# Seven of layer two's weight units multiplied where they were converted, in the first token pair, with a new sequence

## The chip, the cores and the metric

The kernel runs on one core of a Trainium2 chip. The metric is the device time of a run in microseconds (us); the time before is the median of three runs. The engines are named as in the profile: PE is TensorE (PEld its weight loads), DVE is VectorE, ACT is ScalarE, POOL is GpSimd, and SP is SyncE, which here issues all of the DMAs. Each engine works through its own instructions in order.

## The reference, cut to what matters

```python
x = attention(q, k, v)               # 4 x 8 heads, 576 positions, window 32 or 32 x 4, fp32 softmax
x = x.transpose(0, 2, 1, 3).reshape(2304, 512)
h = x @ w_in1                        # layer one: 512 -> 1024
ln = layernorm(h * softmax(h)) * g_ln
y = ln @ w_out1                      # 1024 -> 512
h2 = y @ w_in2                       # layer two: 512 -> 2048
g = h2 / (1 + exp(-1.702 * h2))
out = g @ w_out2                     # 2048 -> 512, all of it fp32 in and out
```

The weights arrive as 64-bit floats and are turned into 32-bit words on the chip.

## The kernel before

Every fp32 product is made from three products of a reduced fp32 type: each operand is split into a high part (`hi`) and the rest (`lo`), and high x high, high x low and low x high are summed.

**Layer two** uses seven block products instead of eight (a Strassen-like scheme). Its 2304 tokens are cut into three *pairs* of 2 x 384 tokens (`p` = 0, 1, 2). The 2048 hidden features are eight *quads* (`q` = 0 to 7). For each pair and quad, `h_prod` (products on line 719, tiles `hx` and `hz`) makes seven products `m` = 0 to 6 of six matmuls each, and `o_prod` (line 796, tiles `ox` and `oz`) does the same for the output side, by `jj` = 0 to 7. The weights of one quad need two *units*, ('q', q, 0) and ('q', q, 1), and each unit has two halves (`part` 0 and 1: 384 and 512 KB). The output side has units ('o', jj, 0) and ('o', jj, 1).

**A unit's way** is: `unit_fetch` (line 629, 512 KB from the input), conversion from 64 to 32 bits (lines 429, 433 or 437, and 441), four sums of blocks (`unit_sum`, line 638), then for each half a `hi` copy (line 655) and a `lo` subtraction (line 659) into an `hl` tile, and `unit_store` (line 663), which writes the half to a DRAM tensor (`wdq`, `wdo`). The products of every pair read the weights back from there: `quad_load` (line 668, tiles `ws`), `o_load` (line 772, tiles `wo`) and `o_load2` (line 782, tiles `w`). The units of groups `PARK[1]` and `PARK[2]` are converted during attention in buffers lent by `y1`; the 23 of `PARK[3]` follow in three `raw` and nine `hl` rooms (six from the end of attention, three more when layer one's first products are done). The same nine `hl` rooms hold the loaded `ws` and `wo` tiles. A quad of pair 0 uses four of them: two units of two halves.

**The order of the work** is written out by hand. `plan.add` collects pieces of work, each with an engine, what it comes after, which rooms it takes and gives back, and a cost. The list `ORDER` numbers the works in the order in which `add` was called and sets the order on every engine; `PICKS` says which engine takes a work that could run on several. The costs (`W2_T` and others) serve the planner; on the chip the order and the semaphores decide. An SP instruction that waits for a room or for a `lo` half holds up all the DMAs behind it.

In pair 0 the quads run in the order 0, 1, 2, 3, 6, 5, 4, 7 on PE, between the last products of layer one (line 599) and the output side. The output side's units 3 come last.

Of the kernel before, what the change touches and what calls it, by code (L numbers as in the profile page):

```python
# [18 lines left out]
P = 128  # L19
# [147 lines left out]
def attention_moe_kernel(ctx, tc, qk, qk_last, v, v_last, masks, w_in, w_out, g_ln, w2_in, w2_out, out):  # L167
# [502 lines left out]
    def quad_weights(q, m, kk, a):  # L670

        part, k = ((0, 2), (1, 1), (1, 2), (1, 0), (0, 0), (0, 1), (1, 3))[m]
        return wst[q, kk, part][:, (2 * k + a) * P:(2 * k + a + 1) * P]
# [35 lines left out]
    def h_prod(p, q, m):  # L709
        if m == 0:  # L710
            hX[q] = [x_tile((p, q, 0), f"hx{p}_{q}_0")]
        elif m == 1:
            hX[q].append(x_tile((p, q, 1), f"hx{p}_{q}_1"))
        elif m in (2, 3):
            hZW[q, m] = psB.tile([P, 512], F32, tag="B", name=f"hz{p}_{q}_{m}")
        ps = hX[q][1 if m == 1 else 0] if m in (0, 1, 4) else hZW[q, 2 if m in (2, 5) else 3]
        for kk in range(2):
            for i, (a, x) in enumerate(((0, 0), (0, 1), (1, 0))):
                nc.tensor.matmul(ps[:, 0:TB2], quad_weights(q, m, kk, a), yc2[m][:, x, kk, :],  # L719
                                 start=(m < 4 and kk == 0 and i == 0), stop=(kk == 1 and i == 2), skip_group_check=True)  # L720
# [29 lines left out]
    def o_block(jj, half, b):  # L750
        return gst[jj, half, b]

    def o_sum(jj, i, eng):

        b11, b12, b21, b22 = (o_block(jj, h, b) for h in range(2) for b in range(2))
        o, x, y_, op = ((b12, b22, b12, ALU.subtract), (b11, b12, b11, ALU.add),
                        (b12, b22, b11, ALU.subtract), (b21, b21, b11, ALU.subtract))[i]
        eng.tensor_tensor(o, x, y_, op)  # L758
# [15 lines left out]
    seen = {}  # L774
# [9 lines left out]
    def o_prod(p, jj, m):  # L784
        k = seen[p, m] = seen.get((p, m), 0) + 1
        first, last = k == 1, k == NQ
# [4 lines left out]
        for d in range(2):  # L791
# [28 lines left out]
    def o_store(p, c):  # L820
        r, b = ((1, 1), (0, 0), (1, 0), (0, 1))[c]
        t = 2 * TB2 * p + TB2 * b
        nc.sync.dma_start(out[2 * P * r:2 * P * r + 2 * P, t:t + TB2].rearrange("(d p) t -> p d t", p=P),
                          ob[c].rearrange("p (d t) -> p d t", d=2))
# [48 lines left out]
    QK_T, V_T, L_T, W_T, W2_T = 1.35, 1.3, 1.45, 1.3, 1.4  # L873
# [119 lines left out]
    stored = {}  # L993
    for k in (1, 2, 3):
        w_after = [end[n] for n in range(4)] if k < 3 else [closed]
        raw, hl = (("raw", k), ("hl", k)) if k < 3 else ("raw", "hl")
        for n, u in enumerate(PARK[k]):
# [5 lines left out]
            w = add(r, "SP", W2_T, fetch, w_after, take=(raw,), lag=3.1)  # L1003
# [6 lines left out]
            for part in range(2):  # L1010
                fin = part == 1

                def split(copy, k=k, u=u, part=part):
# [10 lines left out]
                    r, "SP", W2_T * (1 if fin or u[0] == "o" else 0.77), lambda u=u, p=part: unit_store(u, p), [w], lag=2.0,  # L1024
                    give=(hl,))
# [52 lines left out]
    for p in range(3):  # L1078
# [4 lines left out]
        for n, q in enumerate(QUADS):  # L1083
            r = r0 + 10 * n
            ready, held = [], []
            for kk in range(2):
                for part in range(2):
                    def load(p=p, q=q, kk=kk, part=part):
# [3 lines left out]
                        r - 30, "SP", W2_T * (0.77, 1)[part], load, [stored[("q", q, kk), part], opened] + kept_hi, take=("hl",),  # L1092
# [4 lines left out]
            for m in range(7):  # L1097
# [5 lines left out]
                elif m == 6:  # L1103
                    after.extend(ms[4:])
                w = add(r, "PE", 1.042, lambda p=p, q=q, m=m: h_prod(p, q, m), after,
                        take=(("X", "Q"), ("X",), ("B",), ("B",), (), (), ())[m], give=("hl",) * 4 if m == 6 else ())
# [23 lines left out]
                for key in held if m == 6 else ():  # L1130
                    hl_end[key] = w
# [18 lines left out]
        for jj in range(NQ):  # L1150
            r = r0 + 10 * jj
            loads = []
            for d in range(2):
                def load(p=p, jj=jj, d=d):
                    o_load(jj, d, hl_tile(f"wo{p}_{jj}_{d}", hi_now[p, "o", jj, d], hl_end[p, "o", jj, d]))
                hi_now[p, "o", jj, d] = w = add(
                    r - 60, "SP", W2_T, load, [stored[("o", jj, d), 0], stored[("o", jj, d), 1]] + ready[-1:], take=("hl",),
# [40 lines left out]
        for m in (4, 5, 6):  # L1198
            xs_ = []
            for jj in range(NQ):  # L1200
                r = r0 + 10 * (NQ * (m - 3) + jj)
                if jj % 2 == 0:
# [5 lines left out]
                    hi_now[p, m, jj] = w = add(r - 60, "SP", 1.5, load,  # L1208
# [9 lines left out]
                else:  # L1218
                    last_g[jj, "g11"] = op = operand(jj, m, 1, 1, muls[jj][3:] + [gsum[jj, 0], gsum[jj, 2], now["b21", jj]],
                                                     give=("g11",))  # L1220
                x = add(r, "PE", 1.042, lambda p=p, m=m, jj=jj: o_prod(p, jj, m), [w, op] + wait[m] + end_[3],
                        give=("gs", room) if jj % 2 else ("gs",))
                if jj % 2:
                    x.after.append(xs_[-1])
                hl_end[p, m, jj - jj % 2] = x
                xs_.append(x)
# [5 lines left out]
            else:  # L1232
                cs = []
                for d in range(2):
                    cs.append(add(r, "DVE", 0.56, lambda p=p, c=m - 3, d=d: o_out(p, c, d), xs_ + cs,
                                  take=() if d else ("sg",), give=("B",) if m == 5 else ("B", "p1")))
                store(m - 3, cs)
# [5 lines left out]
def plan_sequence():  # L1243
# [29 lines left out]
    for b in range(1, B):  # L1273
        todo, k = items[b - 1], 0
        for u in range(UB):
# [36 lines left out]
PARK = {1: [('q', 4, 1), ('q', 0, 1), ('q', 3, 1)],  # L1312
# [9 lines left out]
ORDER = [10, 1, 97, 98, 99, 100, 8, 56, 57, 58, 59, 101, 60, 4, 77, 78, 5, 67, 79, 68, 61, 62, 69, 80, 81, 9, 266,  # L1322
# [248 lines left out]
```

## Time and profile before

| | us |
|---|---|
| median of 3 runs | 677.64 (676.11 to 681.71) |
| profiled execution | 675.26 |
| its span, first to last instruction | 673.5 |
| PE busy | 640.5 (95%) |
| DVE, ACT, POOL busy | 440.6, 352.2, 292.6 |
| DMA | 169.99 MB, 252 GB/s over the span |

The span is what the trace covers; the execution's time has a little more around it. A busy PE is not a PE at its peak, because matmuls overlap and their ends are modelled. The granted clock of PE (PEclk) is given as a share of full speed.

### The profile page before, as it was taken

What the parts mean: (1) busy time and instruction counts of PE and PEld (TensorE: products, weight loads), DVE (VectorE), ACT (ScalarE), POOL (GpSimd) and SP (SyncE); (2) the same over time, 40 slices, a digit from 0 to 9 for tenths busy, and PEclk for the clock granted to TensorE, in tenths of its full rate; (3) what the DMA queues carried; (4) which work ended last, traced back from release to release, by engine and by line L of the source; (5) the groups of instructions that cost most, each with busy time, mean ns of one, the idle gap of its engine ahead of it and who ended that gap; (6) DMA issues with size and microseconds to landing.
All of it is one profiled execution on the core that took longest, in us unless ns stands there. A gap on an engine that the chain in (4) does not pass through costs nothing.

```text
span 673.5 us, 14859 instructions
## 1 busy us (share of the span) xinstructions
PE 640.5 (95%) x5877; PEld 596.9 (89%) x5877; DVE 440.6 (65%) x777; ACT 352.2 (52%) x762; POOL 292.6 (43%) x343
## 2 busy tenths in 40 slices
PE   6699999999999999999778899999999999999997
PEld 3467898888998999999678899999999999999997
DVE  4888877866777766866576678643466763354764
ACT  3778867764576466544235556322465542334552
POOL 1345655566344557336135116400665461133464
PEclk9889999999999999999799999999999999999999
DMA  9995753735546756597999999686898777878882
GB/s 336 402 355 177 251 179 138 241 109 191 174 142 213 251 201 247 200 319 254 356 292 367 316 327 311 227 274 232 259 313 281 243 223 241 281 246 267 287 268 102
DMA packets 67013, 169.99 MB, mean 252 GB/s; under 512 B 7168, under 2 KB 28800, under 8 KB 66944
## 3 DMA queue, kind: packets, MB, share of 16 engines
q1 hardware_dynamic: 66944, 169.05, 74.1%
q8 instruction: 46, 0.75, 0.5%
q14 instruction: 23, 0.19, 0.1%
HBM read 132.85 MB, written 36.18 MB: 251 GB/s over the span
## 4 chain that ended last, share of the span: by engine, by line
PE 81%; DMA 9%; DVE 4%; POOL 3%; issue 2%; ACT 1%; SPq 0%; DVEq 0%; POOLq 0%; ACTq 0%
PE y L599 15%; PE h L522 15%; PE oz L796 13%; PE hz L719 11%; PE ox L796 9%; PE hx L719 8%; DMA ws<-wdq 4%; PE lt L577 2%; DMA wo<-wdo 2%; PE s L268 2%; PE ptp L351 1%; POOL gs L765 1%; PE xt L381 1%; DMA wdo<-hl_('o', 5, 1)_0_4980 1%; PE xt L384 1%
## 5 line engine op out<-in xcount | busy, mean ns | idle before, releaser
L762 ACT CAST gs<-g 128x384 fp32r<-128x384 f32 x168 | 85.1, 514 | 75.6 <-PE ox L796 27.0
L765 POOL TENSOR_TENSOR gs<-g,gs 128x384 fp32r<-128x384 f32 x64 | 69.6, 1096 | 106.5 <-ACT gs L762 91.1
L719 PE MATMUL hz<-yc,ws 128*128 128x384 f32 x576 | 112.0, 336 | 1.6 <-POOL yc L706 0.7
L719 PEld LDWEIGHTS hz<-yc,ws 128*128 128x128 f32 x576 | 101.4, 189 | 2.6 <-POOL yc L706 1.1
L719 PE MATMUL hx<-yc,ws 128*128 128x384 f32 x432 | 88.2, 342 | 10.3 <-DMA ws<-wdq 10.2
L765 DVE TENSOR_TENSOR gs<-g,gs 128x384 fp32r<-128x384 f32 x104 | 68.1, 669 | 43.8 <-ACT gs L762 43.0
L719 PEld LDWEIGHTS hx<-yc,ws 128*128 128x128 f32 x432 | 76.9, 192 | 13.0 <-DMA ws<-wdq 9.2
L599 PE MATMUL y<-lnh,wo_h 128*128 128x256 f32 x288 | 82.5, 287 | 0.0
L599 PE MATMUL y<-lnl,wo_h 128*128 128x256 f32 x288 | 81.4, 283 | 0.0
L599 PE MATMUL y<-lnh,wo_l 128*128 128x256 f32 x288 | 81.4, 283 | 0.0
L748 ACT ACTIVATE g<-g 128x384 f32<-128x384 f32 x72 | 36.6, 522 | 62.7 <-DVE g L738 30.6
L758 POOL TENSOR_TENSOR g<-g,g 128x384 f32<-128x384 f32 x31 | 34.4, 1113 | 70.2 <-ACT g L748 51.1
L522 PE MATMUL h<-wi_h,xh 128*128 128x512 f32 x144 | 58.9, 409 | 0.5 <-issue 0.5
L796 PE MATMUL ox<-gs,wo 128*128 128x384 f32 x288 | 56.2, 339 | 3.0 <-DMA wo<-wdo 2.8
L522 PE MATMUL h<-wi_l,xh 128*128 128x512 f32 x144 | 56.3, 391 | 0.0
L522 PE MATMUL h<-wi_h,xl 128*128 128x512 f32 x144 | 56.3, 391 | 0.0
L599 PEld LDWEIGHTS y<-lnh,wo_h 128*128 128x128 f32 x288 | 55.1, 191 | 0.5
L599 PEld LDWEIGHTS y<-lnl,wo_h 128*128 128x128 f32 x288 | 55.2, 192 | 0.3
L599 PEld LDWEIGHTS y<-lnh,wo_l 128*128 128x128 f32 x288 | 55.1, 191 | 0.0
L796 PEld LDWEIGHTS ox<-gs,wo 128*128 128x128 f32 x288 | 50.0, 188 | 5.3 <-issue 2.7
L796 PE MATMUL oz<-gs,wo 128*128 128x384 f32 x288 | 54.7, 336 | 0.0
L796 PE MATMUL oz<-gs,w 128*128 128x384 f32 x288 | 53.9, 337 | 0.0
(343 smaller groups left out, 1250.4 us busy)
## 6 DMA issues: line engine op xcount, KB each, us to landing
ws<-wdq SPq DMA_DIRECT2D x48, 512.0 KB, 6.0
wo<-wdo SPq DMA_DIRECT2D x48, 512.0 KB, 5.9
ws<-wdq SPq DMA_DIRECT2D x48, 384.0 KB, 5.4
w<-wdo SPq DMA_DIRECT2D x72, 256.0 KB, 5.8
qk<-in_qk_dram SPq DMA_DIRECT2D x14, 528.0 KB, 5.1
v<-in_v_dram SPq DMA_DIRECT2D x14, 512.0 KB, 5.7
y<-in_w_in_dram SPq DMA_DIRECT2D x9, 512.0 KB, 4.8
wdq<-y SPq DMA_DIRECT2D x9, 512.0 KB, 6.5
```

What stands on the lines that cost most here:

```text
L268: nc.tensor.matmul(ps[QB * j:QB * j + QB, h, m * KW:m * KW + KW], q_[rows, c:c + QB], k_[rows, c:c + KW], start=not masked, stop=not maske ...
L351: nc.tensor.transpose(ps[:, j * P:j * P + P], t[:, 2 * j:2 * j + 2, :].rearrange("p m k -> p (m k)"), ident)
L381: nc.tensor.matmul(o, w, pt[rows, x:x + QB].rearrange("p (r t) -> p r t", r=4), start=True, stop=True, tile_position=(64 * par, 64 * h))
L522: nc.tensor.matmul(hps[i][:, half, :], x[:, kt, :], w[:, kt, fs], start=(kt == 0 and j == 0), stop=(kt == KT - 1 and j == 2))
L577: nc.tensor.transpose(ps[:, j, :], es[i][:, f * P:f * P + P], ident)
L599: nc.tensor.matmul(yps[g, dm][:, 0:n], w[:, f, ds_], x[:, f, 0:n], start=(f == 0 and j == 0), stop=(f == NF1 - 1 and j == 2))
L719: nc.tensor.matmul(ps[:, 0:TB2], quad_weights(q, m, kk, a), yc2[m][:, x, kk, :], start=(m < 4 and kk == 0 and i == 0), stop=(kk == 1 and i ...
L748: nc.scalar.activation(g_tile(q, 0, 0) if (half, b) == (0, 0) else src, src, AF.Gelu_apprx_sigmoid)
L758: eng.tensor_tensor(o, x, y_, op)
L762: nc.scalar.copy(gsp[jj, m][:, 0], o_block(jj, half, b))
L765: eng.tensor_tensor(gsp[jj, m][:, 1], o_block(jj, half, b), f32(gsp[jj, m][:, 0]), ALU.subtract)
L796: nc.tensor.matmul(ps, w, gsp[jj, m][:, x], start=m < 4 and first and i == 0, stop=last and i == 2, skip_group_check=True)
```

## The change

The seven units ('q', 1, 1) to ('q', 7, 1) are listed in `KEPT`. In pair 0 the products read their halves from the `hl` tiles in which they were split; they are still stored, since pairs 1 and 2 load them. A kept room is given back when the quad's last product and the store are both done. `PARK` is dealt anew: the units ('q', q, 0) and ('q', 0, 1) come in the lent buffers, and `PARK[3]` holds all the `o` units and the seven kept ones. The loads of `wo` in pair 0 no longer come after the last `ws` load of the planner's list. In the last pair, the last output product (`m` = 6) is cut for `jj` from 4 on: first all of `d` = 0, then all of `d` = 1, and its result is stored in two halves. The planner's costs for DMAs are set anew and `ORDER` and `PICKS` are other lists.

```diff
-    def quad_weights(q, m, kk, a):
+    def quad_weights(p, q, m, kk, a):
         part, k = ((0, 2), (1, 1), (1, 2), (1, 0), (0, 0), (0, 1), (1, 3))[m]
+        if p == 0 and ("q", q, kk) in KEPT:
+            return hls[("q", q, kk), part][:, (2 * k + a) * P:(2 * k + a + 1) * P]
         return wst[q, kk, part][:, (2 * k + a) * P:(2 * k + a + 1) * P]
...
-    def o_store(p, c):
+    def o_store(p, c, d0=0, nd=2):
         r, b = ((1, 1), (0, 0), (1, 0), (0, 1))[c]
-        t = 2 * TB2 * p + TB2 * b
-        nc.sync.dma_start(out[2 * P * r:2 * P * r + 2 * P, t:t + TB2].rearrange("(d p) t -> p d t", p=P),
-                          ob[c].rearrange("p (d t) -> p d t", d=2))
+        t, e = 2 * TB2 * p + TB2 * b, (2 * r + d0) * P
+        nc.sync.dma_start(out[e:e + nd * P, t:t + TB2].rearrange("(d p) t -> p d t", p=P),
+                          ob[c].rearrange("p (d t) -> p d t", d=2)[:, d0:d0 + nd])
...
-    QK_T, V_T, L_T, W_T, W2_T = 1.35, 1.3, 1.45, 1.3, 1.4
+    QK_T, V_T, L_T, W_T, W2_T = 1.35, 1.3, 1.45, 1.3, 1.45
...
                 stored[u, part] = hl_end[u, part] = x = add(
-                    r, "SP", W2_T * (1 if fin or u[0] == "o" else 0.77), lambda u=u, p=part: unit_store(u, p), [w], lag=2.0,
-                    give=(hl,))
+                    r, "SP", 1.35 if fin or u[0] == "o" else 1.1, lambda u=u, p=part: unit_store(u, p), [w], lag=2.1,
+                    give=() if u in KEPT else (hl,))
+                split_of[u, part] = w
...
                 for part in range(2):
+                    u = "q", q, kk
+                    if p == 0 and u in KEPT:
+                        ready.append(split_of[u, part])
+                        held.append((u, part))
+                        continue
...
                 for key in held if m == 6 else ():
-                    hl_end[key] = w
+                    hl_end[key] = w if len(key) == 4 else add(r, None, 0, lambda: None, [w, stored[key]], give=("hl",))
...
-                    r - 60, "SP", W2_T, load, [stored[("o", jj, d), 0], stored[("o", jj, d), 1]] + ready[-1:], take=("hl",),
+                    r - 60, "SP", W2_T, load, [stored[("o", jj, d), 0], stored[("o", jj, d), 1]] + (ready[-1:] if p else []), take=("hl",),
...
+                if p == 2 and m == 6 and jj >= NQ // 2:
+                    for d in range(2):
+                        x = add(r + 100 * d, "PE", 0.521, lambda p=p, m=m, jj=jj, d=d: o_prod(p, jj, m, (d,)),
+                                [w, op] + wait[m] + end_[3] + xs_[:1] + by_d[0][-1:],
+                                give=(("gs", room) if jj % 2 else ("gs",)) if d else ())
...
+                if by_d[0]:
+                    s0 = add(r, "SP", 0.7, lambda p=p, c=m - 3: o_store(p, c, 0, 1), cs[:1], lag=3.0)
+                    add(r, "SP", 0.7, lambda p=p, c=m - 3: o_store(p, c, 1, 1), cs[1:] + [s0], give=("sg",), lag=3.0)
...
-PARK = {1: [('q', 4, 1), ('q', 0, 1), ('q', 3, 1)],
-        2: [('q', 4, 0), ('q', 3, 0), ('q', 1, 0), ('q', 2, 1), ('q', 6, 0), ('q', 5, 0)],
-        3: [('q', 0, 0), ('q', 7, 1), ('q', 7, 0), ('q', 5, 1), ('q', 2, 0), ('q', 1, 1), ('o', 0, 0), ('o', 0, 1),
...
+PARK = {1: [('q', 0, 0), ('q', 0, 1), ('q', 1, 0)],
+        2: [('q', 2, 0), ('q', 3, 0), ('q', 4, 0), ('q', 5, 0), ('q', 6, 0), ('q', 7, 0)],
+        3: [('o', 0, 0), ('o', 4, 1), ('o', 1, 0), ('o', 2, 1), ('o', 0, 1), ('q', 1, 1), ('o', 6, 0), ('o', 7, 0), ('o', 6, 1),
...
+KEPT = [('q', q, 1) for q in range(1, 8)]
```

`ORDER` and `PICKS` are replaced as a whole (2435 works before, 2440 after) and are not shown.

## Rows read from the trace of the kernel before

**Rows 1.** The page, busy tenths of PE and DMA in 40 slices.

```profile
PE   6699999999999999999778899999999999999997
DMA  9995753735546756597999999686898777878882
```

**Rows 2.** Windows: from:to length, busy us by engine, PEclk, DMA share, GB/s.

```profile
0.00:41.92 41.92, 29.68 (x832) 19.79 (x833) 28.77 (x50) 24.97 (x64) 11.24 (x16) 0.88 0.98 369
41.92:302.77 260.85, 259.44 (x3077) 233.60 (x3072) 194.91 (x350) 167.08 (x367) 140.09 (x195) 1.00 0.60 207
302.77:400.82 98.05, 84.33 (x454) 80.16 (x454) 65.59 (x123) 42.97 (x87) 31.57 (x39) 0.97 0.94 317
400.82:669.57 268.75, 267.00 (x1521) 263.39 (x1521) 150.75 (x255) 117.17 (x246) 109.66 (x96) 1.00 0.78 257
669.57:673.50 3.93, 0.00 (x1) 0.00 (x0) 0.60 (x2) 0.00 (x0) 0.00 (x0) 1.00 0.28 100
```

**Rows 3.** Longest wait of PE on loads: total us, times, longest.

```profile
PE hx L719 <- DMA ws<-wdq: 10.2, 7, 4.0
```

**Rows 4.** Timeline of PE: start, length, instruction, idle before.

```profile
302.77 1.20 PE L719 MATMUL hx<-yc,ws 128*128 128x384 f32 x6
303.81 1.20 PE L719 MATMUL hz<-yc,ws 128*128 128x384 f32 x6
331.48 4.21 PE L719 MATMUL hx<-yc,ws 128*128 128x384 f32 x12 [4.00 <-DMA ws<-wdq]
400.82 0.79 PE L796 MATMUL ox<-gs,wo 128*128 128x384 f32 x3 [0.54 <-DMA wo<-wdo]
```

**Rows 5.** Windows inside the stretch of layer two's first pair.

```profile
320.00:337.00 17.00, 12.12 (x53) 11.17 (x52) 8.49 (x17) 4.48 (x9) 1.85 (x4) 0.80 1.00 357
354.00:371.00 17.00, 15.09 (x85) 14.28 (x84) 11.16 (x21) 8.92 (x18) 9.40 (x12) 1.00 1.03 363
```

**Rows 6.** The chain that ended last: start, length, what.

```profile
316.81 0.92 DVE raw_('o', 4, 0)_4435 L638
319.52 6.89 DMA wdo<-hl_('o', 4, 0)_0_4715
326.42 5.01 DMA ws<-wdq
349.93 7.97 DMA wdo<-hl_('o', 5, 1)_0_4980
357.92 4.38 DMA ws<-wdq
```

**Rows 7.** DMA issues of the page, and all landings of L668.

```profile
ws<-wdq SPq DMA_DIRECT2D x48, 512.0 KB, 6.0
DMA to landing us min/median/max: 3.3/5.7/9.1
```

**Rows 8.** Timeline: fetch, first and last conversion of unit ('o', 3, 1).

```profile
358.81 0.37 SPq L629 DMA_DIRECT2D raw_('o', 3, 1)_5070<-in_w_out_dram  x1
365.32 0.68 ACT L437 ACTIVATE raw_('o', 3, 1)_5070<-raw_('o', 3, 1)_5070 128x512 uint32<-128x512 uint8 x1 [0.45 <-DMA raw_('o', 3, 1)_5070<-in_w_out_dram]
372.77 0.69 DVE L659 TENSOR_TENSOR hl_('o', 3, 1)_1_5208<-raw_('o', 3, 1)_5070,hl_('o', 3, 1)_1_5208 128x512 fp32r<-128x512 f32 x1
```

**Rows 9.** Groups by line, 300 to 400 us: two `lo` halves on DVE.

```profile
L659 DVE TENSOR_TENSOR hl_('o', 4, 0)_0_4715<-raw_('o', 4, 0)_4435,hl_('o', 4, 0)_0_4715 128x512 fp32r<-128x512 f32 x1 | 1.4, 1395 | 0.0
L659 DVE TENSOR_TENSOR hl_('o', 5, 0)_0_4882<-raw_('o', 5, 0)_4683,hl_('o', 5, 0)_0_4882 128x512 fp32r<-128x512 f32 x1 | 0.7, 684 | 0.0
```

**Rows 10.** Timeline: the last products and the last two drains.

```profile
656.57 13.00 PE L796 MATMUL oz<-gs,w 128*128 128x384 f32 x72
669.09 1.08 DVE L818 TENSOR_TENSOR ob<-oz,op 128x384 f32<-128x384 f32 x2 [3.41 <-PE oz L796]
```

**Rows 11.** The start: a window, and the last `lo` that gates layer one.

```profile
17.00:34.00 17.00, 11.88 (x338) 8.65 (x335) 14.05 (x25) 12.09 (x32) 5.43 (x5) 0.87 1.03 399
33.76 2.40 POOL L491 TENSOR_TENSOR wi_l<-w1r,wi_h 128x1024 fp32r<-128x1024 f32 x1 [3.53 <-DVE wi_h L478]
```

More of the change, by code (lines that the diff above doesn't have):

```diff
@@ L718, in h_prod @@
             for i, (a, x) in enumerate(((0, 0), (0, 1), (1, 0))):
-                nc.tensor.matmul(ps[:, 0:TB2], quad_weights(q, m, kk, a), yc2[m][:, x, kk, :],
+                nc.tensor.matmul(ps[:, 0:TB2], quad_weights(p, q, m, kk, a), yc2[m][:, x, kk, :],
                                  start=(m < 4 and kk == 0 and i == 0), stop=(kk == 1 and i == 2), skip_group_check=True)
@@ L753, in o_sum @@
     def o_sum(jj, i, eng):
-        b11, b12, b21, b22 = (o_block(jj, h, b) for h in range(2) for b in range(2))
+        b11, b12, b21, b22 = ((h, b) for h in range(2) for b in range(2))
         o, x, y_, op = ((b12, b22, b12, ALU.subtract), (b11, b12, b11, ALU.add),
                         (b12, b22, b11, ALU.subtract), (b21, b21, b11, ALU.subtract))[i]
-        eng.tensor_tensor(o, x, y_, op)
+        eng.tensor_tensor(o_block(jj, *o), o_block(jj, *x), o_block(jj, *y_), op)
     def o_hi(p, jj, m, half, b):
@@ L782, in o_load2, with o_prod @@
             nc.sync.dma_start(f32(t[:, k]), wd["o", jj + k].rearrange("p (d c) -> p d c", d=2)[:, :, at_:at_ + 2 * P])
-    def o_prod(p, jj, m):
-        k = seen[p, m] = seen.get((p, m), 0) + 1
-        first, last = k == 1, k == NQ
+    def o_prod(p, jj, m, ds=(0, 1)):
+        for d in ds:
+            seen[p, m, d] = seen.get((p, m, d), 0) + 1
+        first, last = seen[p, m, ds[0]] == 1, seen[p, m, ds[0]] == NQ
         if first and m < 2:
@@ L790, in o_prod @@
             oZ[m] = [psB.tile([P, 512], F32, tag="B", name=f"oz{p}_{m}_{d}") for d in range(2)]
-        for d in range(2):
+        for d in ds:
             ps = (oX[1 if m == 1 else 0][d] if m in (0, 1, 4) else oZ[2 if m in (2, 5) else 3][d])[:, 0:TB2]
@@ L990, in attention_moe_kernel @@
     ended = add(-1, None, 0, end_y, list(yc.values()))
-    stored = {}
+    stored, split_of = {}, {}
     for k in (1, 2, 3):
@@ L1002, in fetch @@
                     [P, 1024], F32, tag="raw", bufs=NRAW, name=f"raw_{u}")).bitcast(U32))
-            w = add(r, "SP", W2_T, fetch, w_after, take=(raw,), lag=3.1)
+            w = add(r, "SP", 1.6, fetch, w_after, take=(raw,), lag=3.2)
             if w2[u[0]].dtype == I64:
@@ L1091, in attention_moe_kernel @@
                     hi_now[p, q, kk, part] = w = add(
-                        r - 30, "SP", W2_T * (0.77, 1)[part], load, [stored[("q", q, kk), part], opened] + kept_hi, take=("hl",),
+                        r - 30, "SP", (1.15, 1.45)[part], load, [stored[("q", q, kk), part], opened] + kept_hi, take=("hl",),
                         lag=3.0)
@@ L1105, in attention_moe_kernel @@
                 w = add(r, "PE", 1.042, lambda p=p, q=q, m=m: h_prod(p, q, m), after,
-                        take=(("X", "Q"), ("X",), ("B",), ("B",), (), (), ())[m], give=("hl",) * 4 if m == 6 else ())
+                        take=(("X", "Q"), ("X",), ("B",), ("B",), (), (), ())[m], give=("hl",) * sum(len(k) == 4 for k in held) if m == 6 else ())
                 ms.append(w)
@@ L1198, in attention_moe_kernel @@
         for m in (4, 5, 6):
-            xs_ = []
+            xs_, by_d = [], ([], [])
             for jj in range(NQ):
@@ L1207, in load @@
                                 stage[0].tile([P, 1024], F32R, tag="raw", bufs=NRAW, name=f"w2_{p}_{m}_{jj}"))
-                    hi_now[p, m, jj] = w = add(r - 60, "SP", 1.5, load,
+                    hi_now[p, m, jj] = w = add(r - 60, "SP", 1.6, load,
                             [stored[("o", jj + k, d), part] for k in range(2) for d in range(2) for part in range(2)] +
@@ L1220, in attention_moe_kernel @@
                                                      give=("g11",))
[L1221 to L1224, printed above, removed]
+                if p == 2 and m == 6 and jj >= NQ // 2:
[3 more added lines that the diff above has]
+                                give=(("gs", room) if jj % 2 else ("gs",)) if d else ())
+                        by_d[d].append(x)
+                        if d and jj % 2:
+                            x.after.append(by_d[1][-2])
+                else:
+                    x = add(r, "PE", 1.042, lambda p=p, m=m, jj=jj: o_prod(p, jj, m), [w, op] + wait[m] + end_[3],
+                            give=("gs", room) if jj % 2 else ("gs",))
+                    if jj % 2:
+                        x.after.append(xs_[-1])
+                    xs_.append(x)
                 hl_end[p, m, jj - jj % 2] = x
-                xs_.append(x)
             if m == 4:
@@ L1234, in attention_moe_kernel @@
                 for d in range(2):
-                    cs.append(add(r, "DVE", 0.56, lambda p=p, c=m - 3, d=d: o_out(p, c, d), xs_ + cs,
+                    cs.append(add(r, "DVE", 0.56, lambda p=p, c=m - 3, d=d: o_out(p, c, d), xs_ + by_d[d] + cs,
                                   take=() if d else ("sg",), give=("B",) if m == 5 else ("B", "p1")))
-                store(m - 3, cs)
+                if by_d[0]:
+                    s0 = add(r, "SP", 0.7, lambda p=p, c=m - 3: o_store(p, c, 0, 1), cs[:1], lag=3.0)
+                    add(r, "SP", 0.7, lambda p=p, c=m - 3: o_store(p, c, 1, 1), cs[1:] + [s0], give=("sg",), lag=3.0)
+                else:
+                    store(m - 3, cs)
         if p < 2:
@@ L1311 @@
 PTB = 2
-PARK = {1: [('q', 4, 1), ('q', 0, 1), ('q', 3, 1)],
[4 rows of a table removed]
+PARK = {1: [('q', 0, 0), ('q', 0, 1), ('q', 1, 0)],
+        2: [('q', 2, 0), ('q', 3, 0), ('q', 4, 0), ('q', 5, 0), ('q', 6, 0), ('q', 7, 0)],
+        3: [('o', 0, 0), ('o', 4, 1), ('o', 1, 0), ('o', 2, 1), ('o', 0, 1), ('q', 1, 1), ('o', 6, 0), ('o', 7, 0), ('o', 6, 1), ('o', 4, 0), ('q', 2, 1), ('q', 5, 1), ('o', 5, 0), ('o', 3, 1), ('o', 3, 0), ('q', 6, 1), ('q', 4, 1), ('o', 5, 1), ('o', 7, 1), ('o', 2, 0), ('q', 3, 1), ('o', 1, 1), ('q', 7, 1)]}
+KEPT = [('q', q, 1) for q in range(1, 8)]
 PARK_AT = {1: 4, 2: 9, 3: 9}
@@ L1321 @@
 ULO_ANY = True
-ORDER = [10, 1, 97, 98, 99, 100, 8, 56, 57, 58, 59, 101, 60, 4, 77, 78, 5, 67, 79, 68, 61, 62, 69, 80, 81, 9, 266,
[124 rows of a table removed]
-PICKS = {50: 1, 65: 1, 66: 1, 73: 1, 75: 1, 76: 1, 81: 1, 85: 1, 86: 1, 107: 1, 125: 1, 157: 1, 170: 1, 192: 1,
[25 rows of a table removed]
+ORDER = [1, 8, 56, 57, 58, 5, 67, 68, 59, 60, 61, 0, 69, 70, 71, 46, 47, 10, 18, 87, 88, 89, 72, 73, 9, 266, 267, 268,
[125 rows of a table added]
+PICKS = {63: 1, 73: 1, 75: 1, 91: 1, 106: 1, 107: 1, 127: 1, 128: 1, 138: 1, 146: 1, 159: 1, 160: 1, 179: 1, 192: 1,
[23 rows of a table added]
 _INS = ["qk", "qk_last", "v", "v_last", "masks", "w_in", "w_out", "g_ln", "w2_in", "w2_out"]
```

299 rows, old and new, of tables (ORDER, PARK, PICKS) are left out of this document.

## The prediction

> **What bounds the kernel now.** I read the 40 slices first. PE is busy nine tenths or more of nearly every slice; the gaps are at the very start, in the middle (slices 20 to 24) and in the last slice, and in the middle the DMA row stands at 9 [rows 1]. The windows put sizes on that: in the 260.85 us of attention and layer one PE idles 1.41 us, in the 268.75 us after layer two's first pair has got going 1.75 us, but in the 98.05 us between them, from quad 1's first product to the last late `wo` load, it idles 13.72 us at a DMA share of 0.94 [rows 2]. There PE mostly waits for `ws`, the loads of the quad weights [rows 3].
>
> What would that stretch cost without waits? Consecutive products of six matmuls start 1.04 us apart [rows 4]; 454 matmuls [rows 2] are 75.7 products, at 1.042 us 78.8 us. So 98.05 - 78.8 = **19.2 us** are excess: 13.7 of idle PE, about 2.1 because twelve matmuls behind a 4.00 us wait took 4.21 us and not two steps, 2.08 [rows 4], the granted clock being 0.80 in that window [rows 5] (a mean of its 2.4 and 1.2 GHz levels), and some 3.4 of smaller bubbles.
>
> The chain says why. A late unit is split into rooms that a finished quad left, its store takes 6.89 us to land, only then may a `ws` load take the room, 5.01 us more; once again 7.97 and 4.38 [rows 6]. From 316.81 to 331.43 that is 14.6 us, while seven products of one quad cover 7.3. And all of it passes through one queue moving 357 to 363 GB/s at a DMA share of 1.00 to 1.03 [rows 5].
>
> **The change part by part.** The order list names works by the order in which `add` is called; numbering them so, before and after, gives every count below.
>
> *Kept units.* Seven units lose 14 reload DMAs of pair 0: 7 x (393 + 524 KB) = 6.42 MB. Their fetches and stores stay, since pairs 1 and 2 still load them. Between quad 1's last load and `wo` 3's last, SP issued 24 quad loads, 16 `wo` loads, 17 stores and 6 fetches, 31.46 MB; now 11, 16, 21 and 8, 27.66 MB (ten stores of `o` halves move ahead of the stretch, the fourteen of the kept halves into it). Over 98.05 us the old bytes are 321 GB/s, near the window's 317 [rows 2]. At 317 the new ones need 87.2 us, at the 363 of the best window [rows 5] 76.2, under the 76 products now in the stretch (76 x 1.042 + 0.5 for the half product = 79.7). So bytes alone leave an excess of 0 to 7.5 us.
>
> By the Trainium skill, HBM Reference, Specifications (TRN2), a core streaming alone reaches about 425 GB/s, which would need an estimated 65 us for these bytes and leave no excess, as in rival (a); this trace's stretch never shows it, 399 being the most in any window I took [rows 11].
>
> *Rooms.* There are nine, a quad uses four. Of the 14 kept halves, twelve now get rooms left by earlier products and two by stores of an `o` unit issued long before; the ordinary loads wait for the product two quads earlier plus a kept store issued about a quad before that. So the serial store-then-load of 11.9 to 12.4 us [rows 6] no longer lies between two quads; what does is one load, median 6.0 us for 512 KB, 3.3 to 9.1 over all [rows 7], plus two issues of about 0.4 [rows 8], against 7.3. Per quad that is nothing at the median, and 9.1 + 0.8 - 7.3 = 2.6 us at worst; I take 1.0, nearer the median, for six quads 6 us, and 1 us for `wo` 3, whose unit is still fetched last. Excess after: 7, bounds 0 and 7 x 2.6 = 18. Gain 19.2 - 7 = **12.2 us**, bounds 1 and 19. The 2.1 us of clock are in it, as I expect no wait as long as that one.
>
> *Conversion.* What hid a late unit's conversion was its store and reload; now the product waits for it. The unit ('o', 3, 1) took from issue at 358.81 to its last `lo` at 373.46, 14.65 us [rows 8]. In the list the fetches of quads 1, 2, 3, 6, 5, 4, 7 stand 17.8, 19.4, 20, 14.7, 13.5, 15.7 and 22 us of PE work ahead of their first products. Only quad 5 is short, by 1.1 us; that lies in the 7. Price if the cover is gone: the rival below.
>
> *SP's queue.* The kept stores wait for `lo` on DVE or POOL, and loads of the next quad queue behind them. Before, `o` stores stood in the same places (17 of them), so I add nothing; bound, the 2.6 per quad above.
>
> *The last products.* Four jj of the last pair's final product run first all for d = 0, then for d = 1, and the last store is halved. Now PE ends at 669.57, two drains of 0.54 follow to 670.17 [rows 10], and the store fills the rest to 673.5, 3.3 us [rows 2]. One drain (0.54) goes under PE; half the store saves between nothing and 1.7, I take 0.55, since its landing is mostly fixed. **1.1 us**, bounds 0.5 and 2.2.
>
> *The sequence.* At the start the weight chunk that layer one's first product needs comes 15th and not 13th among the loads, 1.6 MB later, at 399 GB/s 4 us [rows 11]; but its `lo` ended at 36.16 [rows 11] and the first layer-one product began at 41.92 [rows 2], so 5.8 us of slack covers it. With 12.24 us of idle PE up to there [rows 2], I take 0, bounds 4 us worse and 3 better. Elsewhere PE idles 3.2 us in 530 [rows 2]: at most that to win; losing is open, the nearest row being a single 4.00 us wait [rows 4]. I take 0. The planner's new costs per DMA reach the chip only through this list.
>
> **Sum:** 12.2 + 1.1 = 13.3 us off 675.26, the profiled execution's own time (span 673.5 and 1.76 around it): 662.0. The median of the runs, 677.64, stands 2.4 above that, so **664.4 us**.
>
> **Rivals.** (a) *Every wait goes.* The loads always land inside 7.3 us, and bytes go at 363. Excess 0 instead of 7: 657; with 2 from the start, 655. For: the median landing. Against: the share of 1.00 and nine rooms.
>
> (b) *The stall is refilled.* Loads of the next quad stand behind kept stores that wait for `lo`, and each store must land before its room is free; what the bytes saved comes back at 2 us a quad and at `wo`, where 13.4 MB are queued between quad 7's last load and `wo` 3's for 35.4 us of PE work (378 GB/s). Excess 14: 19.2 - 14 + 1.1 = 6.3 off, 671.3. For: the 6.89 and 7.97 us of store landings [rows 6].
>
> (c) *Slower: conversion stands in front of every quad.* The list interleaves the kept units' sums and `lo` halves with drains on three in-order engines, and each waits for the others. One `lo` on DVE took 1395 ns and another of the same shape 684 [rows 9]. By the Trainium skill, SBUF — State Buffer, section SBUF: two separate sides, DVE with two SBUF inputs and GpSimd block each other for a whole instruction, which speaks against putting these splits before PE; the 1395 ns would fit it, though no row shows who held the port. Fourteen halves at 0.71 us more are 10 us if none is covered. The rival decides if a conversion takes some 20 us and not 14.65: against leads of 13.5 to 15.7 each stall is 4 to 6 us; if the clock falls behind two of them, as it did behind the 4.00 us wait, that is 2.1 more each [rows 4]. Seven times 4 plus twice 2.1 is 32.2 us against 19.2: 13 slower, less 1.1, 689.5. The point of no gain is 2.9 us per quad. Against it: in this window DVE is idle 5.8 to 8.5 us of 17 [rows 5].
>
> That the change does not do what it says I exclude: `quad_weights` reads the kept tile for p = 0.
>
> **Chances.** Forecast (659 to 669) 0.50, (a) 0.15, (b) 0.23, (c) 0.12. About 1% is what a measurement of this kernel tells from no change: 670.9 to 684.4. Faster: 0.50 + 0.15 + 0.05 of (b) = 0.70; same: 0.18 of (b) and 0.03 of (c), 0.21; slower 0.09. The range runs from 656 to 677: below it about half of (a), above it most of (c).
>
> **What would show it.** In the profile after: 14 fewer `ws` issues; the stretch from quad 1's first product to the last `wo` wait at 84 to 90 us; PE's waits on `ws` at 3 to 6 us where 10.2 stood [rows 3]; no slice of clock below 0.9 in the middle; one drain and a half-size store behind the last matmul. Wrong if PE waits there on DVE, POOL or ACT for `hl` tiles (c), if SP waits for landings of `wdq` ahead of `ws` (b), or if the first layer-one product starts after 44 us.

## The result, and the profile after

The median went from 677.03 us to **659.54 us** (four runs each, 659.26 to 662.58 after); the ratio is 0.9738, 95% interval 0.9685 to 0.9792, and a second comparison with more runs gave 0.9752 (0.9727 to 0.9778). The forecast was 664.4 and faster. The profiled execution of after took 659.48 us, its span is 657.7.

The page first: busy tenths of PE, granted clock and busy tenths of DMA in 40 slices.

```profile
PE   7689999999999999999989989999999999999997
PEclk9889999999999999999999999999999999999999
DMA  8986468544538366967899999658799877679773
```

The 7s and 8s in PE's middle slices [rows 1] have become 8s and 9s, the clock stands at 9 there throughout, and DMA is about as busy as it was. The windows, cut at the same events as [rows 2] (columns as there):

```profile
0.00:41.12 41.12, 28.10 (x801) 17.86 (x801) 28.90 (x45) 23.48 (x63) 11.01 (x15) 0.96 0.96 349
41.12:303.26 262.14, 260.18 (x3098) 233.98 (x3098) 198.18 (x347) 164.77 (x361) 151.45 (x201) 0.99 0.60 203
303.26:387.03 83.77, 80.02 (x458) 78.83 (x457) 65.14 (x122) 47.81 (x98) 35.32 (x38) 1.00 0.93 317
387.03:654.15 267.12, 266.33 (x1524) 264.09 (x1524) 158.10 (x266) 116.35 (x244) 95.38 (x85) 1.00 0.77 258
654.15:657.70 3.55, 0.00 (x0) 0.00 (x0) 0.56 (x1) 0.00 (x0) 0.00 (x0) 1.00 0.45 163
```

The stretch from quad 1's first product to the last `wo` wait fell from 98.05 to 83.77 us at the same 317 GB/s, so its bytes fell from 31.1 to 26.6 MB. One correction: before, the last wait stands ahead of the second half of a product, after, ahead of a whole one, 0.52 us earlier in the work. With that the 15.8 us of span divide so: up to quad 1's first product 0.49 later (layer one begins 0.80 earlier and takes 1.29 longer), the stretch 13.76 shorter, pairs 1 and 2 up to the last drain 1.64 shorter, the end behind it 0.89 shorter.

PE's waits on loads in the middle (total us, times, longest), where 10.2 in 7 stood for `ws` [rows 3]:

```profile
PE hx L721 <- DMA ws<-wdq: 1.8, 2, 0.9
PE ox L799 <- DMA wo<-wdo: 1.9, 2, 1.4
```

The same waits in PE's timeline, and the pieces of the chain of waits that they hang on (start, length, what):

```profile
333.44 0.76 PE L721 MATMUL hx<-yc,ws 128*128 128x384 f32 x3 [0.90 <-DMA ws<-wdq]
342.98 0.77 PE L721 MATMUL hx<-yc,ws 128*128 128x384 f32 x3 [0.95 <-DMA ws<-wdq]
387.03 1.31 PE L799 MATMUL ox<-gs,wo 128*128 128x384 f32 x6 [1.45 <-DMA wo<-wdo]
```

```profile
324.77 8.54 DMA ws<-wdq
335.82 7.03 DMA ws<-wdq
379.81 7.17 DMA wo<-wdo
```

This is the prediction's "one load between two quads": quad 3's last product with one of its halves ends at 324.77 and gives the room, quad 5's load lands in it 8.54 us later, and the products between cover all but 0.90 of that. The pairs of store and load of [rows 6] are gone from this chain. At `wo` 3 the series is still there: before these loads SP waits 3.3 and 0.9 us for the stores of the halves of ('o', 3, 1).

Landing times of the quad loads in the part with the quads (issues, KB, median us), of after and then of before:

```profile
ws<-wdq SPq DMA_DIRECT2D x5, 512.0 KB, 6.6
ws<-wdq SPq DMA_DIRECT2D x6, 384.0 KB, 6.4
```

```profile
ws<-wdq SPq DMA_DIRECT2D x12, 512.0 KB, 7.1
ws<-wdq SPq DMA_DIRECT2D x12, 384.0 KB, 4.9
```

On the whole a load lands no sooner than before: the larger half 0.5 us sooner, the smaller 1.5 us later. What has changed is that one landing, and not two in series, lies between two quads.

### The profile page after: what moved, and what is told of

It is laid out like the page before. It is cut to its first block, busy times and chain, and to the rows that moved or that the text cites. A ratio compares the mean times of both kernels' runs of the same rounds, so it can differ in the third digit from the quotient of the medians.

```text
span 657.7 us, 14874 instructions
## 1 busy us (share of the span) xinstructions
PE 634.6 (96%) x5877; PEld 594.8 (90%) x5877; DVE 450.9 (69%) x779; ACT 352.4 (54%) x765; POOL 293.2 (45%) x338
## 4 chain that ended last, share of the span: by engine, by line
PE 89%; DMA 5%; DVE 3%; issue 1%; ACT 1%; SPq 0%; POOL 0%; ACTq 0%; POOLq 0%; DVEq 0%
PE y L599 16%; PE h L522 16%; PE oz L799 14%; PE hz L721 14%; PE hx L721 11%; PE ox L799 10%; PE lt L577 2%; DMA ws<-wdq 2%; PE xt L381 2%; PE s L268 1%; PE xt L384 1%; PE ptp L351 1%; DMA w1r<-in_w_in_dram 1%; DMA wo<-wdo 1%; DVE gs L767 1%
## 5 line engine op out<-in xcount | busy, mean ns | idle before, releaser
L767 POOL TENSOR_TENSOR gs<-g,gs 128x384 fp32r<-128x384 f32 x51 | 56.6, 1116 | 114.8 <-ACT gs L764 108.8
L721 PE MATMUL hz<-yc,ws 128*128 128x384 f32 x492 | 97.8, 334 | 0.0
L767 DVE TENSOR_TENSOR gs<-g,gs 128x384 fp32r<-128x384 f32 x117 | 75.6, 664 | 30.5 <-ACT gs L764 29.8
L721 PEld LDWEIGHTS hz<-yc,ws 128*128 128x128 f32 x492 | 86.4, 188 | 0.2 <-issue 0.2
L599 PE MATMUL y<-lnl,wo_h 128*128 128x256 f32 x288 | 81.4, 283 | 0.0
L599 PE MATMUL y<-lnh,wo_l 128*128 128x256 f32 x288 | 81.4, 283 | 0.0
L721 PE MATMUL hx<-yc,ws 128*128 128x384 f32 x369 | 75.0, 335 | 1.8 <-DMA ws<-wdq 1.8
L760 POOL TENSOR_TENSOR g<-g,g 128x384 f32<-128x384 f32 x34 | 38.1, 1126 | 66.0 <-ACT g L750 42.1
L721 PEld LDWEIGHTS hx<-yc,ws 128*128 128x128 f32 x369 | 64.7, 188 | 2.6 <-ACT hl_('q', 7, 1)_0_4957 L655 1.2
```

The lines of the kernel that those rows point to most:

```text
L599: nc.tensor.matmul(yps[g, dm][:, 0:n], w[:, f, ds_], x[:, f, 0:n], start=(f == 0 and j == 0), stop=(f == NF1 - 1 and j == 2))
L721: nc.tensor.matmul(ps[:, 0:TB2], quad_weights(p, q, m, kk, a), yc2[m][:, x, kk, :], start=(m < 4 and kk == 0 and i == 0), stop=(kk == 1 an ...
L760: eng.tensor_tensor(o_block(jj, *o), o_block(jj, *x), o_block(jj, *y_), op)
L767: eng.tensor_tensor(gsp[jj, m][:, 1], o_block(jj, half, b), f32(gsp[jj, m][:, 0]), ALU.subtract)
```

## The experiments

Times are compared by their ratios to the runs of before beside them; "stretch" is quad 1's first product to the last `wo` wait, in the profiled execution.

**The removed bytes put back, with nobody waiting.**

```diff
     quad_load(q, kk, part, ...)
+    if p == 0 and q > 0:
+        c0, c1 = (0, 6 * P) if part == 0 else (6 * P, 14 * P)
+        nc.sync.dma_start(spare[q][:, c0:c1], wd["q", q][:, c0:c1])
```

> The kernel after, with the removed 6.42 MB put back as copies that nobody waits for: behind each of the fourteen `ws` loads of quads 1 to 7 in pair 0 (the halves of the units ('q', q, 0)) the same 384 or 512 KB are copied from DRAM to a DRAM tensor that is never read. No room is taken and no product waits for them; what differs from the reload of before is that they write DRAM and not SBUF. About twelve of them, 5.5 MB, fall into the stretch from quad 1's first product to the last `wo` wait (83.8 us after the change). If the gain came from the bytes, the stretch goes back to (27.66 + 5.5) MB / 363 GB/s = 91 us or more, 7 to 14 us slower in all. If it came from the series of store and load that lay between two quads, the copies only lengthen landings: 0 to 3 us slower.

Measured: ratio 0.9847 (0.9827 to 0.9868), 0.95% or 6.4 us slower than after. The stretch as a window, the landings in it, and PE's wait:

```profile
304.77:394.04 89.27, 83.27 (x457) 80.13 (x456) 64.55 (x122) 47.85 (x98) 34.07 (x37) 0.98 0.98 355
```

```profile
ws<-wdq SPq DMA_DIRECT2D x5, 512.0 KB, 7.9
ws<-wdq SPq DMA_DIRECT2D x6, 384.0 KB, 7.6
```

```profile
PE hx L722 <- DMA ws<-wdq: 3.8, 3, 1.8
```

89.27 us at 355 GB/s are 31.7 MB, about what the stretch of before moved in 98.05 us (97.53 without the half product). So with about the same bytes and without the series the stretch is 8.3 us shorter than before, and putting the bytes back costs 5.5 us of the 13.8. Neither theory alone holds. Two things limit this split. It compares single executions, and the four traces of after's stretch lie between 81.5 and 83.8 us, so the 5.5 may be 5.5 to 7.8. And 1.6 us of it are PE's clock: behind the longest wait, from 339.10 to 342.74, four groups of three matmuls start 0.85 to 0.96 us apart, where 0.52 is usual. How the bytes act is seen in the landings: 7.6 and 7.9 us are above the 7.3 us that seven products cover, 6.4 and 6.6 were below. And 317 GB/s was not the most that the queue could do over such a stretch.

**The kept halves not stored.**

```diff
+    kk = 0 if ("q", q, kk) in KEPT else kk            # quad_load, pairs 1 and 2
...
-    lambda u=u, p=part: unit_store(u, p)
+    lambda u=u, p=part: None if u in KEPT else unit_store(u, p)
```

> The kernel after, without the fourteen stores of the kept halves (6.42 MB less); pairs 1 and 2 read the other unit's halves in their place, of the same sizes, so their output is not the reference's. Kept rooms come free with the product alone. After the change PE waits 0.90 and 0.95 us for the `ws` loads of quads 5 and 4, which are issued when the product two quads earlier ends and land 8.54 and 7.03 us later. If the bytes issued around these loads make them long, both waits go and the run is 2 to 3 us faster. If a load of that kind takes so long in any case, because it is released by that product, both waits stay: 0 to 0.5 us faster. The waits of 0.46 and 1.45 us at `wo` 3 hang on an `o` unit's own store and may stay in either case.

Measured: 0.9727 (0.9711 to 0.9742); the interval overlaps that of after. No wait on `ws` is left, and 1.9 us on `wo`. But the stretch, 81.4 us, is that of two runs below which store everything and whose `ws` waits came to 0 and 0.33 us. The two waits lie so near the edge that they come and go between executions; what the stores cost, 0 to 1.7 us, stays open.

**Conversion made longer.**

```diff
-    eng.tensor_tensor(l_, x, f32(h_), ALU.subtract)
+    for _ in range(2 if u in KEPT else 1):            # second kernel: 4
+        eng.tensor_tensor(l_, x, f32(h_), ALU.subtract)
```

> The kernel after, with each of the fourteen kept `lo` subtractions done twice (the same result): 0.55 to 1.46 us more each on DVE or POOL. In the trace of after the last `lo` of a kept unit ends 4.3 us or more before the product that reads it (quad 3: 316.07 against 320.42). If conversion has that much slack, nothing changes (within 1 us). If conversion stands in front of every quad, as the slower rival has it, each of seven quads starts 1 to 3 us later: 7 us or more slower, with PE waiting on DVE or POOL for `hl` tiles.

> The kernel after, with each kept `lo` done four times: 1.7 to 4.4 us more per half, which for the quads with the least slack (quad 3 with 4.3 us, quad 2 with 4.7) is about all of it. By the theory of slack this is where it turns: 0 to 4 us slower, and PE's first waits on DVE or POOL for `hl` tiles in quads 2, 3 or 6. By the slower rival it is 20 us or more.

Measured: twice, 0.9851 (0.9834 to 0.9869), 1.0% or 6.7 us slower than after; four times, 1.0188 (1.0157 to 1.0220), 29 us slower than after and slower than before. The theory of slack missed both sizes. With `lo` twice PE waits for none of the kept tiles but for `u`, a drain on DVE:

```profile
PE hz L722 <- DVE u L734: 4.1, 4, 1.8
```

The longest of the four, on DVE and then on PE:

```profile
314.47 1.91 DVE L660 TENSOR_TENSOR hl_('q', 3, 1)_0_4643<-raw_('q', 3, 1)_4412,hl_('q', 3, 1)_0_4643 128x384 fp32r<-128x384 f32 x2
...
318.02 1.35 DVE L768 TENSOR_TENSOR gs<-g,gs 128x384 fp32r<-128x384 f32 x1
319.29 1.12 DVE L638 TENSOR_TENSOR raw_('q', 6, 1)_4496<-raw_('q', 6, 1)_4496 128x128 f32<-128x128 f32 x1
...
324.01 1.75 DVE L660 TENSOR_TENSOR hl_('q', 6, 1)_1_4709<-raw_('q', 6, 1)_4496,hl_('q', 6, 1)_1_4709 128x512 fp32r<-128x512 f32 x2
325.68 0.55 DVE L730 TENSOR_TENSOR p<-hx,p 128x384 f32<-128x384 f32 x1
326.26 0.56 DVE L734 TENSOR_TENSOR u<-hz,p 128x384 f32<-128x384 f32 x1
```

```profile
326.88 0.79 PE L722 MATMUL hz<-yc,ws 128*128 128x384 f32 x3 [1.82 <-DVE u L734]
```

The same place in after, on DVE and on PE:

```profile
320.97 1.02 DVE L659 TENSOR_TENSOR hl_('q', 6, 1)_1_4703<-raw_('q', 6, 1)_4494,hl_('q', 6, 1)_1_4703 128x512 fp32r<-128x512 f32 x1
322.25 0.56 DVE L729 TENSOR_TENSOR p<-hx,p 128x384 f32<-128x384 f32 x1 [0.25 <-PE hx L721]
322.84 0.56 DVE L733 TENSOR_TENSOR u<-hz,p 128x384 f32<-128x384 f32 x1
```

```profile
324.06 0.68 PE L721 MATMUL hz<-yc,ws 128*128 128x384 f32 x3
```

In after, `p` still waits 0.25 us for PE, and `u` ends at 323.40, 0.66 us ahead of the product that needs it: 0.9 us is all the room there was. The two `lo` take 1.75 us in place of 1.02, but that is the smaller part of the delay. DVE comes to them 3.04 us later than in after, where PE at this place is only 0.83 us later, so 2.2 us were lost on the way: quad 3's doubled half took 1.91 us where after has 0.55, and two operations that the edit does not touch took 1.35 and 1.12 us where after has 0.55 and 0.28. POOL was doing its own doubled `lo` beside them, from 315.92 to 321.91; no row says whether that is why. So the drains `p` and `u`, which stand behind all this in DVE's order, come late, and PE's next `hz` product waits for `u`. The cover to look at is not only the time from `lo` to the product that reads the tile (4.3 us and more), but also the room in DVE's queue ahead of the next drain. This trace is of the fastest of the four runs: its stretch takes 86.7 us, 3 to 5 us more than after's, where the medians differ by 6.7.

With four `lo` the room runs out in nearly every quad, and twice the tile itself is late too, for 2.5 us in sum:

```profile
PE hz L722 <- DVE u L734: 17.7, 6, 5.0
PE hx L722 <- POOL hl_('q', 5, 1)_1_4844 L660: 1.4, 1, 1.4
PE hz L722 <- POOL hl_('q', 2, 1)_1_4567 L660: 1.1, 1, 1.1
```

```profile
332.43 5.11 DVE L660 TENSOR_TENSOR hl_('q', 6, 1)_1_4721<-raw_('q', 6, 1)_4500,hl_('q', 6, 1)_1_4721 128x512 fp32r<-128x512 f32 x4
```

```profile
335.12 0.69 PE L722 MATMUL hx<-yc,hl_('q', 3, 1)_0_4651 128*128 128x384 f32 x3
...
338.65 1.33 PE L722 MATMUL hz<-yc,ws 128*128 128x384 f32 x3 [2.85 <-DVE u L734]
339.78 1.16 PE L722 MATMUL hz<-yc,hl_('q', 3, 1)_0_4651 128*128 128x384 f32 x3
```

```profile
334.00:351.00 17.00, 14.15 (x66) 13.83 (x65) 11.88 (x19) 4.55 (x9) 10.74 (x11) 0.80 0.58 204
```

The stretch takes 111.3 us. Behind the 2.85 us wait three matmuls last 1.16 us and not 0.69, and the granted clock of the window is 0.80, between the two levels of 2.4 and 1.2 GHz: that part of the price is the clock's. The waits on the tiles came where the theory of slack had put its turning point (quad 2 among them), but the price, 29 us, is the slower rival's.

**The end.** First the last result stored whole, then also the products of both d together.

```diff
-    s0 = add(r, "SP", 0.7, lambda ...: o_store(p, c, 0, 1), cs[:1], lag=3.0)
-    add(r, "SP", 0.7, lambda ...: o_store(p, c, 1, 1), cs[1:] + [s0], ...)
+    s0 = add(r, "SP", 0.7, lambda: None, cs[:1], lag=3.0)
+    add(r, "SP", 0.7, lambda ...: o_store(p, c), cs[1:] + [s0], ...)
... second kernel, also:
-    lambda p=p, m=m, jj=jj, d=d: o_prod(p, jj, m, (d,))
+    lambda p=p, m=m, jj=jj, d=d: None if d else o_prod(p, jj, m)
```

> The kernel after, with the last result stored whole again, behind both drains; the last products still run first for d = 0, then for d = 1. In the trace of after the span ends 3.55 us behind PE's last product, in that of before 3.93 us. The prediction gave the half-size store 0.55 us (0 to 1.7) and the drain under PE 0.54. If that holds, the span ends 4.1 us behind PE here (3.55 + 0.55). If the landing of the store is fixed, nothing changes: 3.5 to 3.6 us.

> The kernel after, with the whole of the last-products edit undone: the products of both d together for every jj, two drains, one store. By the prediction's terms the end lies 3.55 + 0.55 + 0.54 = 4.6 us behind PE's last product, 1.1 us later than after. By the windows of the two traces, 3.93 of before against 3.55, it is only 0.4 us later: 3.9 to 4.0 us behind PE.

Measured: 0.9734 (0.9681 to 0.9787) and 0.9757 (0.9702 to 0.9812), too wide for the question; the traces decide. PE's modelled end is not a good mark here (in before the drains start ahead of it), the start of the drain that waits for the last product is. After, whole store, all undone, in this order:

```profile
654.18 0.56 DVE L821 TENSOR_TENSOR ob<-oz,op 128x384 f32<-128x384 f32 x1 [1.00 <-PE oz L799]
```

```profile
652.62 0.56 DVE L821 TENSOR_TENSOR ob<-oz,op 128x384 f32<-128x384 f32 x1 [1.00 <-PE oz L799]
```

```profile
651.88 1.54 DVE L821 TENSOR_TENSOR ob<-oz,op 128x384 f32<-128x384 f32 x3 [1.52 <-PE oz L799]
```

From 654.18 to the span's end of 657.7 are 3.52 us; from 652.62 to 656.6 with the whole store 3.98: the half store is worth 0.46. The eight other traces here with the halved store give 3.40 to 3.61 us, so this is clear of their scatter. Before it was 4.41, from 669.09 [rows 10] to 673.50, so by difference the drain under PE is worth the other 0.43. The full undo ends 4.2 us behind its drains (653.42 to 657.6) and 5.2 behind PE's modelled end, more than either expectation: in this list a drain and the store of m = 5 also come last. It doesn't restore the end of before and prices nothing alone.

**The kernel before with small loads.**

```diff
-    def quad_load(q, kk, part, hl):
+    def quad_load(q, kk, part, hl, p=1):
...
+    n = n if p else 2
...
+    k = k if p else 0                                 # quad_weights
```

> The kernel before, with the quad loads of pair 0 cut to their first 256 columns (128 KB each, in place of 384 and 512 KB); the products of pair 0 use those columns for every block, so its output is not the reference's. In the stretch from quad 1's first product to the last `wo` wait (98.05 us) 24 such loads move 3.1 MB and not 11.0: 7.9 MB less, more than the change takes out, while the series stays as it was: a late unit's half is stored from the room, the store lands, then the load takes a room. If bytes bound the stretch, it falls to 80 to 84 us (14 to 18 us faster in all). If the series of store and load holds as such, each late quad still waits for a store (6.89 and 7.97 us in before) and a short load of some 3 us, about 10.5 us against 7.3 of products: 1.5 to 3 us a quad stay, and the stretch is 88 to 95 us (3 to 10 us faster).

Measured: 0.9819 (0.9777 to 0.9861), 12.3 us faster than before, between the two expectations. The stretch itself is where the bytes were to put it: from quad 1's first product at 305.50 to the half product at which the stretch of before ends (388.58; the last `wo` wait now lies three products earlier) it takes 83.1 us, 15.0 less than before. The trace reaches quad 1 2.7 us later than that of before, which takes part of the gain back. PE waits nowhere on `ws`; the landings of those loads, and what PE waits for in their place:

```profile
ws<-wdq SPq DMA_DIRECT2D x24, 128.0 KB, 2.4
```

```profile
PE ox L798 <- DMA wo<-wdo: 3.5, 3, 1.4
PE hz L721 <- DVE u L733: 1.2, 3, 0.7
```

The series is still there, but a short load of 2.4 us, behind stores that land in 2.6 to 5.6 us where the same ten took 5.8 to 8.2, nearly fits into 7.3 us. The run shortens both landings along with the bytes, so it does not price the one apart from the other: its 15.0 us are not to be added to the 8.3 and 5.5 above. What it shows is that a series costs by the sum of its landings, which the bytes lengthen; fewer landings or shorter ones both help.

By the Trainium skill, DMA: Bandwidth & Descriptors, section Anatomy of one DMA — SWDGE (gpsimd) path, a transfer that GpSimd issues costs about 2.0 us and its bytes at 436 GB/s: an estimated 2.3 us for 128 KB and 3.2 for 512 KB. Here SP issues the loads; the 2.4 us for 128 KB agree all the same, but of the 384 and 512 KB loads only the quickest, 3.3 [rows 7], comes near the estimate, and in this stretch the median of the 512 KB loads, 6.6 to 7.1 us, is twice it.

**After once more, and an eighth kept unit.** The first is the kernel after, unchanged. The second also keeps ('o', 3, 1); the third has the same eight units and a list searched anew.

```diff
-KEPT = [('q', q, 1) for q in range(1, 8)]
+KEPT = [('q', q, 1) for q in range(1, 8)] + [('o', 3, 1)]
...
+    if m < 4 and p == 0 and ("o", jj, d) in KEPT:     # o_prod
+        n = 6 + a if k == 0 else 2 * k - 2 + a
+        w = hls[("o", jj, d), int(k > 0)][:, n * P:n * P + P]
```

> The kernel after as it is, for a narrower ratio and a second trace beside the runs below: 0.974 of before. In the runs with the same code in the stretch the waits on the `ws` loads of quads 5 and 4 were 1.85, 0 and 0.33 us in sum, those at `wo` 3 1.4 to 1.9; a fourth trace should lie in these ranges, with a stretch of 81 to 84 us.

> The kernel after with an eighth kept unit: ('o', 3, 1), the last to be converted, is read by pair 0's products of jj = 3 from the `hl` tiles; its store stays, one `wo` load (512 KB) goes, its two rooms are held until jj = 3 is done. The list is that of after, with the numbers shifted. If the wait at the last `wo` load (1.0 to 1.6 us in every trace of after's code) comes from the unit's own series of store and load, it shrinks to 0 to 0.5 us: 0.7 to 1.5 us faster than after. If the held rooms matter more, the `w` loads of m = 4 come late and PE waits for them: 0 to 2 us slower.

> The same eight kept units with a list searched anew from the start of layer two's conversions on, by the planner's costs with longer landings (3.3 us for stores, 3.6 for loads) beside its own. By those costs it is 0.5 to 2 us ahead of the one above; if the costs miss what the chip does in DVE's queue, it is 0 to 3 us behind.

Measured: 0.9752 (0.9727 to 0.9778), 0.9761 (0.9737 to 0.9784), 0.9809 (0.9772 to 0.9846). After once more, the stretch is 83.08 us, with 1.3 us of waits on `ws` and 1.4 on `wo`. With the eighth unit the wait at jj = 3 is gone, and another stands in its place:

```profile
383.06 1.28 PE L803 MATMUL ox<-gs,wo 128*128 128x384 f32 x6 [1.37 <-DMA wo<-wdo]
```

By the order list that is the load of jj = 5. In the chain it starts at 376.52, when a product ends and gives a room, and lands 6.41 us later; the two rooms now held are the likely reason, which no run tests. A wait is passed on, and no time gained. The list searched with longer landings is 3 to 4 us behind both. So no version here beats the kernel after.

**Nothing kept.** Dealing, end and costs of after, the fourteen reloads put back, the list searched by the planner's costs.

```diff
-KEPT = [('q', q, 1) for q in range(1, 8)]
+KEPT = []
```

> The kernel after with no kept unit: dealing, tail and planner's costs as after, the fourteen reloads put back, the list taken from after with each reload behind its store and then searched for an hour by the planner's costs. These put it 14 us behind after and 2 to 6 us behind before. If the new dealing and sequence alone made the gain, it is within 3 us of after. If the kept units made it, it is 670 us or more, with PE waiting on `ws` as in before.

Measured: 0.9993 (0.9968 to 1.0017), the time of before, 16 us behind after. PE's waits in the middle, and the first such series in its chain:

```profile
PE hx L721 <- DMA ws<-wdq: 7.3, 5, 4.2
PE hz L721 <- DMA ws<-wdq: 3.8, 3, 2.8
```

```profile
307.39 7.29 DMA wdq<-hl_('q', 2, 1)_1_4551
314.74 5.07 DMA ws<-wdq
319.85 1.33 PE hz L721 x3
```

A store of 7.29 us and a load of 5.07 in series, as in [rows 6]. New dealing and sequence alone bring nothing with this list, though a better one may exist; with the lists at hand the kept units bring the gain.

## Why the prediction was right, and where its sizes were off

**What bounds the kernel.** Right: 13.76 of the 15.8 us came from the stretch named. But I counted its work by the 454 matmuls on record. Some are missing from the trace; the list has 76.5 products there, 79.7 us, so the excess before was 18.3 and not 19.2.

**Kept units.** Fourteen fewer `ws` issues (82 in the page, 96 before), and the stretch at 83.77 us, just under the 84 to 90 forecast. The bounds for bytes alone, 76.2 to 87.2 us, held.

**Rooms.** The mechanism was right, its size too large, and this is the mis-sized term of the sum. I took 7 us of excess: 1.0 for each of six quads and 1 at `wo` 3. The list has 76 products between the two marks, 79.2 us, so the excess is 4.6 in after; in the three other traces with this stretch unchanged it is 3.9, 2.3 and 2.4 (83.08, 81.48 and 81.63 us). At most two of the six quads wait, 0 to 1.9 us in sum where I forecast 3 to 6, since the median landing of 6.4 to 6.6 us is under 7.3; I gave the worst landings too much weight. That the gain came within 1.6 us of my 12.2 is in part luck: an excess before that was 0.9 too large hid part of the 2.4 by which the excess after was too large. At `wo` the waits are 1.4 to 1.9 us. No fall of clock followed, as forecast.

**Conversion.** PE waits for no `hl` tile in after, as forecast, and quad 5, the one short by 1.1 us in my count, had its last `lo` done at 331.13, 6 us ahead of its reader. But I measured the cover by the wrong lead. Rival (c) said that the engines in order would wait for each other and put its point of no gain at 2.9 us a quad; doubling the `lo`, 1.3 to 2.6 us a quad on its engines, already costs 6.7 us; the trace shows it coming through DVE's queue and not through the tile. The kernel sits nearer to that rival than my 0.12 and its "conversion of 20 us" let appear. I also priced the rival wrongly: against the leads I listed, a conversion of 20 us is short for quads 1, 2, 6, 5 and 4 by 18.9 us in sum, not by 4 for each of seven. What the Trainium skill (SBUF — State Buffer, section SBUF: two separate sides) says of DVE and GpSimd blocking each other is still not shown here: the doubled `lo` of DVE averaged 0.7 to 1.5 us for 512 columns where 0.68 stands undisturbed, but no row names the holder of the port.

**SP's queue.** Right at nothing: in after SP waits there for rooms and `lo` halves, but for landings of `wdq` nowhere.

**The last products.** 1.1 forecast, 0.89 measured: 0.46 for the half store (0.55), 0.43 for the drain (0.54).

**The sequence.** At the start 0 forecast, 0.49 later, inside the bounds; layer one's first product began at 41.12, not after 44. Elsewhere I took 0 of at most 3.2 us; 1.64 were gained. Of that 0.83 are waits of PE (1.50 before, 0.67 after); the rest is in bubbles that I did not trace.

**The step to the median.** I added 2.4 us because the median of before stood that far above its profiled execution. After, the two are 659.54 and 659.48. It was scatter, not a property: in the other comparisons the medians of before were 674.98 to 677.01. So the miss of 4.9 us, which left 659.54 just inside the lower end of my 659 to 669, is 2.4 from here and 2.5 from the sum (stretch 1.56, pairs 1 and 2 1.64, less 0.21 and 0.49).

**Rivals.** (a), at 657, came nearer in time than the forecast, but not by its mechanism alone: two traces with this stretch show it almost without `ws` waits, yet `wo` 3 still waits in all, and an excess of 2.3 to 4.6 us is left where (a) had none. (b) would have needed landings above 7.3 us, which the copies produced. (c) needs about three more `lo` per half to lose to the kernel before.

## What to carry to other kernels

Where a room goes from product to load to product, compare the sum of the landings in series with the work that covers it: here, by two traces, taking one transfer out of that series paid some 8 us and the bytes it moved some 5.5. When an operation is put ahead of a product, look for what is queued behind it on its own engine: here drains that DVE reached late, with 0.9 us of room, stopped PE for up to 1.8 us, and the tile itself never did until the work was four times as long. And set a forecast against the same kind of number as the result: one execution's distance to a median of three is noise.

## What had not been expected of the hardware

With 4.5 MB fewer in the stretch, loads landed no sooner (6.4 to 6.6 against 4.9 to 7.1 us) and the rate stayed at 317 GB/s; with copies that nobody waited for it rose to 355.

The length of a wait alone does not tell whether the granted clock falls. Behind 1.82 us with `lo` twice, the matmuls ran on at the full level, 0.52 us for each three. With the copies they fell to about half of that pace for some 3.6 us, shortly after a wait of 1.80 us, and the window reads 0.90:

```profile
334.00:351.00 17.00, 15.05 (x77) 14.47 (x76) 10.92 (x22) 6.18 (x13) 7.43 (x10) 0.90 0.99 365
```

The landings vary from execution to execution enough to make 0.9 us waits appear and vanish with the same code: 0 to 1.9 us of `ws` waits in four traces.
